# Sliding attention and soft MoE on one core: w1 of experts 0 to 2 loaded as 112 rows and small parts

## The chip, the cores and the metric

The kernel runs on one core of one Trainium2 chip. The metric is the device time of the whole program in microseconds (us), median of several runs, smaller is better. The core's engines go by the profile's names: PE (matmul), PEld (weight load of PE), DVE (vector), ACT (scalar), POOL (GpSimd) and SP (sync). Its transfers are carried by 16 DMA engines.

## The reference

Attention over 8 batches, 8 heads, 576 positions and 64 columns for each head, with two kinds of mask, and behind it a soft mixture of 8 experts with 4 slots each:

```python
def _attn_ref(q, k, v):                       # (8, 8, 576, 64)
    scores = scale * np.matmul(q, k.transpose(0, 1, 3, 2))
    rel = pos[:, None] - pos[None, :]
    mask_plain = (rel >= 0) & (rel < 32)
    mask_dil = (rel >= 0) & (rel < 128) & (rel % 4 == 0)
    ...                                       # heads 0-3 plain, 4-7 dilated
    attn = softmax(where(masks, scores, -1e9))
    return np.matmul(attn, v)

def _moe_ref(x, phi, w1, w2):                 # x (4608, 512), phi (512, 32)
    logits = x @ phi
    d = softmax over rows (axis 0);  slot_input = d.T @ x      # (8, 4, 512)
    for e in range(8):                        # w1 (8, 512, 1024), w2 (8, 1024, 512)
        h = np.maximum(slot_input[e] @ w1[e], 0.0)
        slot_out[e] = h @ w2[e]
    c = softmax over slots (axis 1)
    return c @ slot_out                       # (4608, 512), float32
```

All inputs are float32 in HBM.

## The kernel before, in words

Every large transfer is issued from POOL and turns float32 into float16 on its way in (or float16 into float32 on its way out). One transfer of queries, keys or values is one batch of one of them: 128 partitions of 4608 bytes in float16 (`load_raw`, L197). It lands in a `raw` tile, DVE turns it in blocks of 32 x 32 (L231), and from there on the batch goes through a software pipeline of four stages.

The order of the instructions is written out by hand: `ORDER` (L48) is a list of steps, each with the stage that it belongs to, and the main loop (L540) runs over 11 rounds and in each over the steps. A step such as `S0.0` computes a group of scores, `E0.0` its exponentials on ACT, `MK0.1` the masks on DVE, `AP4.2` the product with the values, `LG.2` and later the logits and the sums of the mixture. Nothing reorders them later; each engine runs its part of this list in order, and waits on semaphores where it needs another's result.

Loads follow the same list. When the second turning step of Q, K or V of batch b is written, `loads` (L527) issues the transfer of batch b + 2 into the tile that has come free. Behind V of batches 3 to 7 one item of `EARLY` (L149) is issued: w1 of expert 0, 1, 2, 3 and 4, each with one transfer (`load_full`, L205). Behind V of batch 7 w1 of experts 5 to 7 and w2 of experts 0 to 2 follow at once. When the last scores are done, w2 of experts 3 to 5 and four pairs of halves of w2 of experts 6 and 7 (`load_half`, L216) are issued into memory that has come free.

A tile of w1 for an expert has 128 partitions. Partition p holds two pieces of 2048 values (u = 0 and u = 1), each of two rows of w1 one behind the other:

```python
in_=moe_w1[e0:e1].rearrange("e (u p c) f -> p (e u) (c f)", u=2, p=128)
```

So a "row" of such a transfer, here and below, is one partition: two runs of 8 KB of float32 in HBM, 4 KB of float16 in the tile.

After the last batch, PE multiplies the slots with w1 (L608), then with w2 (L641). The output is made in halves of columns: `emit_batch` (L681) multiplies with the combine weights (L664), scales on ACT (L673) and DVE (L677), and stores 512 KB at a time (L686); the left-over rows are stored at the end (L713). The first output half needs the first column half of w2 of all experts, the second one the rest.

Transfers use eight completion semaphores in turn; each transfer adds 16 to its semaphore, in 16 steps whose times stand in the trace.

Of the kernel before, what the change touches and what calls it, by code (L numbers as in the profile page):

```python
# [10 lines left out]
FP16 = mybir.dt.float16  # L11
# [16 lines left out]
N_SLOTS = 32  # L28
# [68 lines left out]
def kernel(  # L97
# [10 lines left out]
    nc = tc.nc  # L108
# [5 lines left out]
    consts = ctx.enter_context(tc.tile_pool(name="consts", bufs=1))  # L114
# [3 lines left out]
    ident = cst[:, o : o + 128]  # L118
    spread = cst[:, o + 128 : o + 256]
    quad = cst[:, o + 256 : o + 260]  # L120
    masks = consts.tile([128, NMASK], FP16, name="masks")
    phi_raw = consts.tile([128, 4, N_SLOTS], FP16, name="phi_raw")
    phi4 = consts.tile([128, 4, 4, N_SLOTS], FP16, name="phi4")
# [14 lines left out]
    def weights_tile(pool, which, e0, e1):  # L138
        n = (4 * FDIM, 8 * DMODEL)[which - 1]
        t = pool.tile([128, e1 - e0, n], FP16, name=f"w{which}_{e0}", tag=f"w{which}_{e0}")  # L140
        for e in range(e0, e1):
            of = t[:, e - e0]
            if which == 1:
                w1t[e] = of.rearrange("p (c f) -> p c f", c=4)
            else:
                w2t[e] = of.rearrange("p (c n) -> p c n", c=8)
        return t

    EARLY = [(1, e, e + 1) for e in range(5)] + [(1, 5, 8), (2, 0, 3)]  # L149
    early_tiles = {x: weights_tile((w1_pool, w2a_pool)[x[0] - 1], *x) for x in EARLY}  # L150
# [46 lines left out]
    def load_raw(which, b):  # L197
        t = raw_pool.tile([128, PJ * D], FP16, name=f"raw{which}_{b}", tag=f"raw{which}")
        raw[(which, b)] = t
        src = {"Q": q, "K": k, "V": v}[which][b]  # L200
        nc.gpsimd.dma_start(  # L201
            out=t, in_=src.rearrange("(g h) (p j) d -> (h p) g (j d)", g=2, j=PJ)
        )

    def load_full(t, which, e0, e1):  # L205
        if which == 1:
            nc.gpsimd.dma_start(
                out=t.rearrange("p e (u x) -> p (e u) x", u=2),
                in_=moe_w1[e0:e1].rearrange("e (u p c) f -> p (e u) (c f)", u=2, p=128),
            )  # L210
        else:
            nc.gpsimd.dma_start(
                out=t, in_=moe_w2[e0:e1].rearrange("e (p c) n -> p e (c n)", p=128)
            )

    def load_half(e, s, n):  # L216
# [253 lines left out]
    for which in "QK":  # L470
        load_raw(which, 1)
    nc.gpsimd.dma_start(
        out=phi_raw.rearrange("p (u c) s -> p u (c s)", u=2),
        in_=moe_phi.rearrange("(u p c) s -> p u (c s)", u=2, c=2),
# [8 lines left out]
    def load_weights(n):  # L483
        for _ in range(n):
            x = weights.pop(0)
            load_full(early_tiles[x], *x)

    tmp = {}

# [36 lines left out]

    def loads(which, b):  # L527
        load_raw(which, b)
        if which == "V":
            if b > 2:  # L530
                load_weights(1)
            if b == B - 1:
                load_weights(len(weights))

    frees = {}
# [4 lines left out]
    for it in range(B + max(s for _, s in STEPS)):  # L540
        for op, stage in STEPS:
            b = it - stage
            if not 0 <= b < B:
                continue
            step(op, b)
            if op in frees and b + 2 < B:
                loads(frees[op], b + 2)
            left.discard((op, b))
            if w2b_pool is None and not left:
                raw_pool.release()  # L550
                w2b_pool = tc.alloc_tile_pool(name="w2b", bufs=1, side="right")
                late = weights_tile(w2b_pool, 2, 3, 6)
                slab_weights(6, "qk0", QK_SLAB)
                slab_weights(7, "qk1", QK_SLAB)
                load_full(late, 2, 3, 6)
                for s in range(2):
                    for e in (6, 7):
                        load_half(e, s, 8 if e == 6 else 4)
        if it == 0:
            nc.vector.tensor_copy(  # L560
                out=phi4, in_=phi_raw[:, :, None, :].broadcast_to([128, 4, 4, N_SLOTS])
            )
# [40 lines left out]
    for fc in range(2):  # L603
        for g in range(2):
            for dc in range(4):
                for j in range(4):
                    e = 4 * g + j
# [9 lines left out]
    for c in range(8):  # L617
# [3 lines left out]
        out=hTm[:, 0].rearrange("p c (j s) -> p c j s", j=4)[:, :, :, 0:16], in_=hT4[:, :, :, 0:16]  # L621
    )
    nc.scalar.copy(
        out=hTm[:, 1].rearrange("p c (j s) -> p c j s", j=4)[:, :, :, 16:32], in_=hT4[:, :, :, 16:32]
# [87 lines left out]
    for e in range(2):  # L712
        nc.gpsimd.dma_start(  # L713
            out=rest[:, e, 512:576, :].rearrange("n i d -> i n d"), in_=om_l[64 * e : 64 * e + 64]
# [37 lines left out]
```

## Time and profile before

| | |
|---|---|
| time, median of 3 runs | 178.32 us (178.19 to 178.39) |
| time of the profiled execution | 178.29 us |
| its span | 176.5 us |
| busy: PE, PEld, DVE, ACT, POOL | 123.5, 80.9, 126.0, 123.5, 38.4 us |
| DMA packets | 18981, 40.83 MB as they land, mean 231 GB/s |
| HBM read, written | 62.07 MB, 9.44 MB |
| one transfer of Q, K or V | 576 KB landed, 11.4 to 12.7 us from issue to landing (medians) |
| one transfer of w1 of one expert | 1024 KB landed, 15.9 us from issue to landing |
| outputs in half columns | 512 KB each, 4.6 us from issue to landing |

The span is the time from the first to the last instruction in the profiled execution; the run's time has 1.8 us more around it. The time from issue to landing holds the time in the queue. Bytes are counted as they land, so a weight of float32 counts half of what is read for it. Engines are counted busy only while they compute, or, on POOL, while it writes the descriptors of a transfer.

### The profile page before, as it was taken

To read this page: it belongs to the slowest core of one execution; us is meant where nothing else is said; L and a number is where in the kernel's file an instruction comes from. 1 tells how busy PE (TensorE), PEld (TensorE's weight loads), DVE (VectorE), ACT (ScalarE), POOL (GpSimd) and SP (SyncE) were. 2 spreads that over 40 slices of the span, in tenths; PEclk is the share of its full clock that TensorE was granted. 3 is DMA by queue.
4 is the path that set the end of the run, shared out by engine and by line. 5 is a ranking of instruction groups with operands and counts; after the bars stand their busy time and mean duration, and the time that the engine had idled before them with its cause. 6 is when DMAs were issued, how large, how long until landed. Compare 5 with 4: busy or idle time off the path is not lost.

```text
span 176.5 us, 4724 instructions
## 1 busy us (share of the span) xinstructions
PE 123.5 (70%) x2004; PEld 80.9 (46%) x2004; DVE 126.0 (71%) x275; ACT 123.5 (70%) x266; POOL 38.4 (22%) x60
## 2 busy tenths in 40 slices
PE   0026928998888888988989888978677295778300
PEld 0015616676566566656766557656332142221000
DVE  6473899999999999999999998465130104878500
ACT  6007758999999999999999999995501104888300
POOL 7321022112112112116000002710000001856600
PEclk9999999969999999999789999996858969655555
DMA  5999999999999999999999999999999999999997
GB/s 83 215 214 210 214 212 215 215 213 214 216 212 217 211 218 215 208 215 220 213 211 217 213 218 216 222 210 225 213 213 221 192 198 175 340 398 397 401 415 209
DMA packets 18981, 40.83 MB, mean 231 GB/s; under 512 B 1169, under 2 KB 11537, under 8 KB 18193
## 3 DMA queue, kind: packets, MB, share of 16 engines
q0 software_dynamic: 18816, 40.41, 113.8%
q8 instruction: 15, 0.25, 0.5%
q1 hardware_dynamic: 144, 0.14, 0.3%
q14 instruction: 6, 0.04, 0.1%
HBM read 62.07 MB, written 9.44 MB: 405 GB/s over the span
## 4 chain that ended last, share of the span: by engine, by line
ACT 38%; DMA 27%; DVE 14%; PE 10%; issue 2%; POOL 2%; POOLq 0%; ACTq 0%
DMA w<-in_moe_w_dram 19%; ACT p L282 10%; DMA phi_raw<-in_moe_phi_dram 8%; ACT vX L253 7%; ACT xp L337 7%; DVE qk L231 5%; PE f L664 5%; ACT om L673 3%; ACT xT L376 3%; ACT xT L378 3%; DVE p L293 3%; DVE vT L231 3%; ACT xd L337 2%; PE s L273 2%; PE rp L357 2%
## 5 line engine op out<-in xcount | busy, mean ns | idle before, releaser
L282 ACT ACTIVATE p<-s 128x1920 f16<-128x1920 f32 (+1 forms) x24 | 44.6, 1857 | 10.2 <-PE s L273 10.1
L273 PE MATMUL s<-qk 32*128 32x128 f16 (+2 forms) x704 | 26.7, 295 | 18.4 <-DVE qk L231 12.0
L253 ACT COPY vX<-rv 128x768 f16<-128x768 f16 (+1 forms) x32 | 27.8, 943 | 1.8 <-PE rv L247 1.8
L316 PEld LDWEIGHTS <-p 128*128 128x128 f16 (+1 forms) x480 | 22.4, 103 | 13.3 <-DVE xp L341 4.0
L337 ACT ACTIVATE xp<-o_P,rc_P 128x64 f16<-128x64 f32 x96 | 26.5, 497 | 2.2 <-DVE rc_P L328 2.2
L273 PEld LDWEIGHTS <-qk 32*128 32x128 f16 x704 | 17.3, 117 | 21.6 <-DVE qk L231 12.0
L293 DVE TENSOR_TENSOR p<-p,masks 128x1920 f16<-128x1920 f16 (+1 forms) x24 | 25.7, 1084 | 0.2
L231 DVE STREAM_TRANSPOSE qk<-rawQ 128x576 uint32<-128x576 uint32 x16 | 18.8, 1243 | 2.7 <-DMA rawQ<-in_q_dram 2.7
L316 PE MATMUL o_P<-vX,p 128*128 128x65 f16 (+1 forms) x288 | 20.0, 205 | 0.8 <-ACT xp L337 0.2
L231 DVE STREAM_TRANSPOSE qk<-rawK 128x576 uint32<-128x576 uint32 x16 | 19.5, 1231 | 0.4 <-DMA rawK<-in_k_dram 0.4
L247 PE MATMUL rv<-cst,vT 128*128 128x128 f16 x176 | 17.5, 242 | 3.2 <-DVE vT L231 1.8
L231 DVE STREAM_TRANSPOSE vT<-rawV 128x576 uint32<-128x576 uint32 x16 | 19.4, 1223 | 0.5 <-DMA rawV<-in_v_dram 0.5
L686 POOL DMA_DIRECT2D out_dram<-om x15 | 11.1, 744 | 39.2 <-DVE om L677 34.8
L247 PEld LDWEIGHTS <-vT 128*128 128x128 f16 x176 | 13.2, 124 | 7.5 <-issue 3.7
L677 DVE TENSOR_SCALAR om<-f,rrow 128x256 f16<-128x256 f32 (+1 forms) x28 | 13.5, 519 | 3.5 <-PE f L664 2.9
L664 PE MATMUL f<-so_sb,ET 32*128 32x256 f16 (+1 forms) x60 | 12.5, 392 | 3.9 <-ACT om L673 2.7
L673 ACT ACTIVATE om<-f,rrow 128x256 f16<-128x256 f32 (+1 forms) x28 | 12.8, 503 | 2.6 <-PE f L664 2.0
L376 ACT COPY xT<-rp 128x576 f16<-128x576 f16 x16 | 11.5, 909 | 1.3 <-PE rp L357 1.3
L316 PE MATMUL o_D<-vX,p 128*128 128x65 f16 x128 | 9.9, 202 | 2.5 <-DVE xp L341 2.0
L201 POOL DMA_DIRECT2D rawQ<-in_q_dram x8 | 5.1, 633 | 29.4 <-DVE rc_P L328 18.4
L378 ACT COPY xT<-rd 128x576 f16<-128x576 f16 x16 | 10.6, 795 | 0.0
L341 DVE TENSOR_TENSOR xd<-o_D,rc_D 128x256 f16<-128x256 f32 x24 | 9.9, 412 | 0.2
(81 smaller groups left out, 176.7 us busy)
## 6 DMA issues: line engine op xcount, KB each, us to landing
w<-in_moe_w_dram POOLq DMA_DIRECT2D x3, 3072.0 KB, 35.5
out_dram<-om POOLq DMA_DIRECT2D x11, 512.0 KB, 4.6
w<-in_moe_w_dram POOLq DMA_DIRECT2D x5, 1024.0 KB, 15.9
rawQ<-in_q_dram POOLq DMA_DIRECT2D x8, 576.0 KB, 12.7
rawK<-in_k_dram POOLq DMA_DIRECT2D x8, 576.0 KB, 11.4
rawV<-in_v_dram POOLq DMA_DIRECT2D x8, 576.0 KB, 11.6
out_dram<-om POOLq DMA_DIRECT2D x2, 1024.0 KB, 7.3
w<-in_moe_w_dram POOLq DMA_DIRECT2D x2, 512.0 KB, 36.7
```

The source lines that it names most:

```text
L231: nc.vector.transpose(out=out_, in_=in_)
L247: nc.tensor.transpose(rg[:, n_t, :, c, :], rows, ident)
L253: copy(out=vX[b % 2][:, t0 : t0 + n, :, 0:D], in_=rg.rearrange("p n h c d -> p n h (c d)"))
L273: nc.tensor.matmul(sps[:, h, c0 : c0 + w], kk, qq, start=(tt == 0), stop=(tt == 1))
L282: return nc.scalar.activation(out=pt, in_=sps[:, :, 0:n], func=AF.Exp, scale=SCALE)
L293: return nc.vector.tensor_tensor(out=pt, in0=pt, in1=m, op=ALU.mult)
L316: nc.tensor.matmul(o[rows, h, :], lhs, rhs, start=(n == 0), stop=(n == len(jobs) - 1), skip_group_check=True,)
L337: nc.scalar.activation(out=dst[:, h], in_=src[:, h], func=AF.Copy, scale=rc[:, h : h + 1])
L376: copy(out=xT_t[b][:, c, :], in_=rg[:, 0:S])
L378: copy(out=xT_t[b][:, 2 + c, :].rearrange("p (i r) -> p i r", r=DIL), in_=rg[:, :, 0:SUB].rearrange("p r i -> p i r"),)
L664: nc.tensor.matmul(fp[:, 0 : c1 - c0], ET[32 * j : 32 * j + 32, m : m + 128], so_sb[32 * j : 32 * j + 32, c0:c1], start=True, stop=True,)
L673: nc.scalar.activation(out=dst, in_=fp[:, 0 : c1 - c0], func=AF.Copy, scale=rrow[:, blk : blk + 1])
```

## The change

w1 of experts 0, 1 and 2 is no longer one transfer each. `load_pieces` issues the first 112 partitions as one transfer, and for expert 0 also the half u = 1 of the other 16. What remains is put on a list, `pieces`, from which `loads` takes one each time that it has issued a transfer of Q, K or V:

- expert 0: the halves u = 0 of partitions 112 to 127, in four transfers of 8, 4, 2 and 2 partitions, behind Q, K and V of batch 4 and Q of batch 5
- expert 1: partitions 112 to 119 and 120 to 127, behind K and V of batch 5
- expert 2: partitions 112 to 119 behind Q of batch 6 and 120 to 127 behind V of batch 6, and a `step_cursor` after each of them, behind K of batch 6 and Q of batch 7

`step_cursor` loads from eight rows of phi two runs of 32 values each into a new small tile, `aside`, which nothing reads. Every byte of w1 is still loaded once, to the same place.

```diff
+    aside = consts.tile([16, 3, 2, N_SLOTS + 16], FP16, name="aside")
...
+    def step_cursor(i, n):
+        nc.gpsimd.dma_start(
+            out=aside[0:n, i, :, 0:N_SLOTS],
+            in_=moe_phi[0 : 5 * n].rearrange("(p u) s -> p u s", u=5)[:, 0:4:2, :],
+        )
+
+    pieces = []
+
+    def load_pieces(t, e):
+        src = moe_w1[e].rearrange("(u p c) f -> p u (c f)", u=2, p=128)
+        dst = t[:, 0].rearrange("p (u x) -> p u x", u=2)
+        nc.gpsimd.dma_start(out=dst[0:112], in_=src[0:112])
+
+        def piece(p, n, u=None):
+            if u is None:
+                return lambda: nc.gpsimd.dma_start(out=dst[p : p + n], in_=src[p : p + n])
+            return lambda: nc.gpsimd.dma_start(out=dst[p : p + n, u], in_=src[p : p + n, u])
+
+        if e == 0:
+            nc.gpsimd.dma_start(out=dst[112:128, 1], in_=src[112:128, 1])
+            p = 112
+            for n in (8, 4, 2, 2):
+                pieces.append(piece(p, n, 0))
+                p += n
+        elif e == 1:
+            pieces.extend((piece(112, 8), piece(120, 8)))
+        else:
+            pieces.extend(
+                (piece(112, 8), lambda: step_cursor(0, 8), piece(120, 8), lambda: step_cursor(1, 8))
+            )
...
             x = weights.pop(0)
-            load_full(early_tiles[x], *x)
+            if x[0] == 1 and x[1] < 3:
+                load_pieces(early_tiles[x], x[1])
+            else:
+                load_full(early_tiles[x], *x)
...
         load_raw(which, b)
+        if pieces:
+            pieces.pop(0)()
         if which == "V":
             if b > 2:
                 load_weights(1)
             if b == B - 1:
+                while pieces:
+                    pieces.pop(0)()
                 load_weights(len(weights))
```

## The prediction

> **What bounds the kernel now.** I read the sliced page first, to see which resource is busy throughout, then the chain of waits, then the DMA queues, and last the single packets and completions that the trace keeps for each transfer.
>
> ```profile
> DVE  6473899999999999999999998465130104878500
> ACT  6007758999999999999999999995501104888300
> ...
> DMA  5999999999999999999999999999999999999997
> ```
>
> Each digit is a slice of 4.4 us. The DMA engines are at 90% or more in 38 of 40 slices, also where ACT falls off (from slice 27, 119 us).
>
> ```profile
> 109.68 1.62 PE s L273 x24
> 111.30 0.28 issue
> 111.58 0.74 POOL w L220
> 112.33 34.05 DMA w<-in_moe_w_dram
> 146.37 0.04 issue
> 146.41 0.32 PE so L641 x4
> ...
> 165.69 0.65 issue
> 166.34 0.63 POOL out_dram L713
> ```
>
> The chain (start, length, what) spends 34.05 us in one small transfer of w2. It isn't a long transfer: it stands behind the backlog of weights. So from 4 us to 151.7 us the kernel is one stream of loads, and what ends it is the last of 16 DMA engines.
>
> ```profile
> PE so L641 <- DMA w<-in_moe_w_dram: 3.0, 2, 2.3
> ...
> DVE qk L231 <- DMA rawQ<-in_q_dram: 2.7, 1, 2.7
> ```
>
> In the table of waits (total us, times, longest) the compute engines wait for loads only at the very start and for the last weights. V of batch 7 lands at 92.0 us and is first read at 102.7; V of batch 3 lands at 38.3, and its first transpose is at 50.5. Queries, keys and values have over 10 us to spare.
>
> ```profile
> q0 software_dynamic: 18816, 40.41, 113.8%
> q8 instruction: 15, 0.25, 0.5%
> ...
> q14 instruction: 6, 0.04, 0.1%
> ```
>
> The instruction fetches on q8 look like nothing (0.5%), but each is one packet of 16 KB on one engine. Their starts are 22.3, 33.4, 42.7, 48.9, 57.0, 65.0, 72.1, 80.2, 86.1 ... 144.8 us, and they take 0.89 to 1.07 us. The 16 completion times that every transfer leaves show what they do. K of batch 1 (landed 17.9) completes on its 16 engines within 0.41 us. After the first fetch, one engine is 0.7 us behind the rest (26.4 to 27.1); after the eighth, eight are about 1 us behind (82.6 to 83.0 against 81.4 to 82.1). The ninth and later ones hit the same eight again. The last weight transfer completes at 149.0 to 150.2 us on nine engines and at 151.3 to 151.7 on seven. So eight engines carry all the fetches, seven twice, and are up to 2.66 us late; the others are free, and idle until the first output packet at 150.68.
>
> What follows is DMA-bound too: 9.4 MB of output in 512 KB transfers that land every 1.32 us, 4 to 5 us after their issue. The late engines run without a pause from 151.70 to the last landing at 175.23. The span (176.5) ends 1.3 us behind it, and the run's own time is 178.29, 0.03 below the median of three (178.32).
>
> **The change, part by part.**
>
> *Bytes and rows.* Each expert's w1 is 128 rows of two packets (2048 packets of 4096 B for eight experts: 16 on each engine for each expert, eight rows). 112 rows are seven for each engine. What matters is where the other 16 go. For expert 0 the 16 half rows, then 8, 4, 2 and 2 half rows are 16 twice over. If a transfer of n rows takes n engines, and the next one goes on where it stopped, every engine gets its eighth row. Expert 1 with 8 and 8 is the same. Expert 2 differs: 8 rows, then eight rows of phi into a tile that nothing reads, then 8 rows, then phi again. By the same assumption both 8-row parts fall on the same eight engines, which get two rows, and the other eight none. No transfer before shows under 16 engines, so this placement is the unknown; its cases are priced below.
>
> By the Trainium skill ("DMA: Bandwidth & Descriptors", "Why a DMA increments its semaphore by 16 and not by 1"), a GpSimd transfer whose slowest dimension is 8 takes eight consecutive engines from a round-robin cursor, and one with 16 takes all. No run so far shows this.
>
> *Is it the late eight that are spared?* If the first part starts at the first engine, the first eight get more. Which are late isn't named, but the packet list gives a hint. Around 151 us the early engines write 1024-byte output packets while the late ones still load 512-byte ones. Of 23 neighbouring pairs of these two kinds with the same start in ns, the early engine's stands first in 20. A list kept by engine number would give that if the late ones are the upper eight (the one engine of them with a single fetch being nearly on time). So I take it that the upper eight are relieved.
>
> *Price.* In steady state 4096-byte packets start 0.305 us apart on an engine (they take 0.324 and overlap by 0.019). One row less is 2 x 0.305 = -0.61 us on each late engine, +0.61 on the early ones. Reading a row's price from 0.65 (two whole packets) gives -0.65 at most.
>
> *Added transfers.* Expert 0 goes from one to six, expert 1 to three, expert 2 to five: 11 more. Each ends in a completion packet on every engine, 22 ns: eight packets of a Q load at 0.342 and this 22 make 2.758, and loads land 2.76 apart. 11 x 0.022 = +0.24 us. If engines outside a part had no completion it would be five on a late engine, 0.11; with the longest completion packets among loads (42 ns) 0.46. I take 0.24, as all transfers of the trace complete 16 times. The phi steps are two packets each, of the kind that in the phi load start 13 ns apart: 4 x 13 = +0.05 on the engines that are stepped over, the late ones. The phi load itself, 32 KB in small packets, moved the stream by 0.26 us (17.89 to 18.15), so a small transfer in a full queue has no large fixed cost.
>
> Against the change stands a rule of the Trainium skill (same page, "Anatomy of one DMA"): a fixed cost of about 2.0 us for each GpSimd transfer. In series that would be an estimated 22 us more, some 200 us; the phi row speaks against it, since the queue is never empty here.
>
> *POOL.* A load of Q, K or V keeps POOL 0.59 us, one of w1 0.79. Eleven more issues are 6.5 to 8.7 us on an engine that is 22% busy and idle 2.0 to 4.7 us before each load. Each part follows a load; behind it wait the next load, 2 to 5 us away, and on V the weights, 0.6 us later into a backlog of over 8 us. Eight completion semaphores are used in turn, so w1 of expert 1 may have to wait some 1.6 us for expert 0's 112 rows (landing near 43.2); next behind it is Q of batch 5, at 46.5. All of it costs nothing; were that cover gone, it would be 0.6 us for each part. The delayed rows are first used at 130 us.
>
> *Sum.* -0.61 + 0.24 + 0.05 = -0.32 us on the late engines. Next in line are the early ones: the latest of them ends its weights at 150.2, and 0.61 + 0.24 more is 151.07, still before the late ones' 151.38. The last half of w2 for the first output columns lands on late engines (146.37) and comes 0.32 earlier, so the first output issue (149.40) does too, and the whole output stage moves. 178.29 - 0.32 = 177.97; on the median, 178.0. With the bounds, 177.8 to 178.2.
>
> **Rivals.**
>
> *The wrong eight (slower).* If the first 8-row part of expert 2 falls on the late eight, because the upper eight aren't the late ones or the counting doesn't start at the first engine, each late engine gains a row: +0.61 + 0.24 = +0.85, 179.15. It decides at that one transfer. For it: the trace names no engine, and nothing shows where the count stands. Against: the order of the pairs above.
>
> *No shift.* Parts are spread over all engines, or the steps don't step. Then only the added packets are left, +0.24 to +0.29: 178.6. For it: every transfer shown uses all 16 engines.
>
> *Always from the first engine.* If n rows go to engines 0 to n-1 each time, the upper eight lose 0.5 + 1 + 1 = 2.5 rows (-1.52 us), and the first two gain 1.5 + 1 + 1 = 3.5 (+2.13). With completions these two end at 149.0 to 150.2 + 2.37 = 151.4 to 152.6 instead of the late ones' 151.7: 178.0 to 179.2, middle 178.5. The Trainium skill has, in the section named above, an exception of this kind: some direct copies go over all 16 engines with the rounded-up sixteenth of the partitions on each, so that the last ones stay empty.
>
> *Small transfers in series:* far slower; the phi row leaves little for it.
>
> **How the numbers follow.** Forecast case 0.58, wrong eight 0.21, no shift 0.10, from the first engine 0.08, other slower 0.03. 0.2%, about what a measurement of this kernel can tell from no change, is 0.36 us, and the forecast of -0.32 lies just inside. Its two added terms could be smaller, so I give 0.31 of its 0.58 to faster and 0.27 to same. No shift: 0.06 same, 0.04 slower. First engine: 0.02, 0.03, 0.03. Together faster 0.33, same 0.36, slower 0.31. The likeliest case has 177.8 to 178.2 for itself; with no shift and the first engine that is under 8 in 10, so the range reaches into the wrong eight: 177.8 to 179.2.
>
> **What would show it.** Right: the last weight transfer's 16 completions span about 1.5 us instead of 2.66, their last is near 151.4, V of batch 7 lands within 0.4 us of before, the q0 packets grow by 11 x 16 completions (and 32 of phi), and POOL's waits change nothing. Wrong: a span of nearly 4 us (wrong eight), one unchanged at 2.7 with all of it 0.25 later (no shift), two engines alone at the end (first engine), or idle slices in the DMA row.

## The result, and the profile after

The change is slower: 178.82 us (median of 11 runs, 178.67 to 179.76) against 178.36 us for the kernel before (11 runs, 177.99 to 178.45), ratio 1.0034, 95% interval 1.0021 to 1.0047. The forecast was 178.0, a gain of 0.32; it came out as a loss of 0.46. The profiled execution after took 178.94 us (before 178.29) at a span of 177.2 us (before 176.5).

The sliced part of the page and the DMA queues of the changed kernel:

```profile
DMA  5999999999999999999999999999999999999997
```

```profile
q0 software_dynamic: 19168, 40.41, 113.6%
q8 instruction: 15, 0.25, 0.5%
...
q14 instruction: 5, 0.04, 0.1%
```

The load stream is as full as before, with the same 15 instruction fetches on q8. Queue q0 has 352 packets more. 32 are the steps' packets of phi; 176 are the completions of eleven more transfers, 16 each, as forecast. The other 144 were not foreseen: completion packets that short transfers leave beyond sixteen (see the last section).

The chain of work that ended last (start, length, what) and a row of the table of waits (total, times, longest):

```profile
111.20 0.74 POOL w L252
111.95 35.19 DMA w<-in_moe_w_dram
147.13 0.04 issue
147.18 0.32 PE so L680 x4
...
167.06 0.64 POOL out_dram L752
```

```profile
PE so L680 <- DMA w<-in_moe_w_dram: 4.3, 2, 2.9
```

The same transfer of w2 carries the chain. It was issued 0.38 us earlier than before (111.95 against 112.33) and landed 0.76 later (147.13 against 146.37), and PE's longest wait for it grew from 2.3 to 2.9 us. The first output is issued at 150.18 instead of 149.40, and the last landing moves from 175.23 to 175.82, by 0.59. So the loss is there before the output begins; what comes behind only follows.

Where in the stream it is shows in the 16 completions of the last weight transfer, from the trace's completion times (us, sorted):

```
before  149.04 .24 .25 .31 .33 .59 .81 150.18 .22 | 151.27 .29 .38 .42 .43 .50 .70           mean 150.37
after   148.33 .41 149.36 .85 150.00 .45 .51 .52 .66 .72 .78 .96 151.22 .53 | 152.11 .13     mean 150.47
```

The span grew from 2.66 to 3.80 us, instead of shrinking to 1.5. The late group of seven is gone: most engines now end between 149.4 and 151.5. But two stand alone at 152.11 and 152.13, and two are far too early. The mean is only 0.10 later. To that comes a shift that the change didn't make: the twelve transfers of Q, K and V of batches 0 to 3, all landed before any row is moved, complete 0.10 us earlier here than in the trace of before. Counted from its own start of the stream, the mean is 0.20 later, and that is the whole price of eleven more transfers. The work was hardly made longer, it was put on some wrong engines.

POOL around the first parts and expert 1's 112 rows (start, length; in brackets the idle time before and what ended it):

```profile
37.66 0.59 POOL L202 DMA_DIRECT2D rawK<-in_k_dram  x1 [3.03 <-DVE rc_P L360]
38.20 0.56 POOL L233 DMA_DIRECT2D w<-in_moe_w_dram  x1
...
43.16 0.71 POOL L228 DMA_DIRECT2D w<-in_moe_w_dram  x1 [1.82 <-DMA w<-in_moe_w_dram]
46.19 0.59 POOL L202 DMA_DIRECT2D rawQ<-in_q_dram  x1 [2.32 <-DVE rc_P L360]
```

A part costs POOL 0.56 us here, and the new wait for a completion semaphore is there: 1.82 us, ahead of expert 1's 112 rows. Q of batch 5 is issued 3.03 us after it and has to wait for DVE anyway. V of batch 7 lands at 91.9 us (before 92.0). So POOL is not the cause.

### The profile page after: what moved, and what is told of

Read it like the earlier page. It is cut to its first block, busy times and chain, and to the rows that moved or that the text cites. A ratio compares the mean times of both kernels' runs of the same rounds, so it can differ in the third digit from the quotient of the medians.

```text
span 177.2 us, 4744 instructions
## 1 busy us (share of the span) xinstructions
PE 122.4 (69%) x2004; PEld 82.4 (47%) x2004; DVE 125.9 (71%) x275; ACT 123.3 (70%) x266; POOL 44.4 (25%) x71
## 4 chain that ended last, share of the span: by engine, by line
ACT 38%; DMA 28%; DVE 14%; PE 10%; issue 3%; POOL 2%; POOLq 0%; ACTq 0%
DMA w<-in_moe_w_dram 20%; ACT p L314 10%; DMA phi_raw<-in_moe_phi_dram 8%; ACT vX L285 7%; ACT xp L369 7%; DVE qk L263 5%; PE f L703 5%; ACT om L712 3%; ACT xT L408 3%; ACT xT L410 3%; DVE p L325 3%; DVE vT L263 3%; ACT xd L369 2%; PE s L305 2%; PE rp L389 2%
```

## The experiments

The question was which engines get the parts of 2 to 16 rows, and which engines are the late ones. Each ratio is against the kernel before, timed with it on the same chip. "Late engine" means one of the seven that end the last weight transfer at 151.27 to 151.70 before the change. The parts' names (`load_pieces`, `step_cursor`, `piece`) are those of the change; kernels that split one expert leave the others as one transfer. The trace names no engine: the numbers 0 to 15 count from where the first part of whole rows, or the first step, of a kernel falls, and that place is taken to be engine 0.

One thing has to be taken off before completions of two traces are compared. The stream of loads doesn't start at the same time in each execution. "Start" below is the mean completion of the twelve transfers of batches 0 to 3, as a difference to the trace of before; it lies between -0.10 and +0.32 us, and no kernel has moved a row by then. Already the first load of Q completes at 6.60 us (mean of 16) before, at 6.50 with the change and at 6.87 in the kernel with parts on 6 to 13. Completions are given as the traces have them.

**One part of the change at a time, and two checks of placement.** Expert 1 alone:

```diff
-            if x[0] == 1 and x[1] < 3:
+            if x[0] == 1 and x[1] == 1:
```

> Expert 1 alone is split, into 112 rows and two parts of 8 rows; experts 0 and 2 are loaded whole. Theory F (every small part starts at the first engine, so that 8 rows always go to the same lower eight engines): the upper eight lose one row (0.61 us), the lower eight gain one; the last weight transfer's latest completion goes from 151.70 to about 151.1, the early engines end at 150.9 at the latest, and the time is 177.8 (0.6 below before). Theory C (the parts go round the engines, as the forecast had it): balanced, only two more completions, 178.4. Theory N (parts are spread evenly, added transfers cost time): 178.4 as well.

Measured: 178.31 us against 178.33, ratio 1.0001 (0.9992 to 1.0010). The last completions are those of before: nine to 150.36, then seven at 151.27 to 151.64. If both 8-row parts had fallen on the same eight engines, these would have gained a row and the others lost one. So theory F is out: the second part went on where the first had stopped (C), or both were spread over all engines (N), which expert 2 alone rules out below.

Expert 0 alone:

```diff
-            if x[0] == 1 and x[1] < 3:
+            if x[0] == 1 and x[1] == 0:
```

> Expert 0 alone is split, into 112 rows, 16 half rows, and 8, 4, 2 and 2 half rows; experts 1 and 2 are loaded whole. Theory F: the first two engines gain 1.5 rows (0.92 us) and end at 151.3 at the latest, the upper eight lose half a row (0.31): latest completion about 151.5, time 178.15, 0.2 below before. Theory C: all balanced, five more completions, 178.45. Theory N: the same 178.45.

Measured: 178.20 us against 178.33, ratio 0.9991 (0.9982 to 0.9999). The completions are 148.82 to 150.71 on nine engines and 151.05 to 151.30 on seven: the late group came 0.3 earlier, some of the others up to 0.5 later. So expert 0 is not balanced. Its parts are half rows; 0.305 us is just the one packet that a late engine has less if the 8, 4, 2 and 2 half rows all start at the first engine each time, so that they stay on the first eight. That start is inferred; no run shows it engine by engine.

Expert 1 as 112 rows and eight parts of 2 rows:

```diff
-            pieces.extend((piece(112, 8), piece(120, 8)))
+            pieces.extend(piece(p, 2) for p in range(112, 128, 2))
```

> Expert 1 alone is split, into 112 rows and eight parts of two rows, one behind each of the next eight transfers of queries, keys and values. Theory F: the first two engines carry all 16 rows, seven more than their own (+4.3 us), and stand alone at the end of the weights, at 153.5 to 154.7 with all others at 151.1 or before; time 180.2 to 181.4. Theory C: the eight parts go once round the 16 engines, balanced, 178.5. Theory N: 178.5.

Measured: 178.51 us in one run. Completions 149.08 to 150.35 and 151.34 to 151.73: balanced again. This fits eight parts of two whole rows that go once around the sixteen engines. The Trainium skill ("DMA: Bandwidth & Descriptors", "Why a DMA increments its semaphore by 16 and not by 1") has this rule for GpSimd transfers: k consecutive engines from a round-robin cursor. These completions agree with it. Its exception fits the half rows of expert 0 (late group 0.3 us earlier): some direct copies are dealt out over all sixteen engines with the rounded-up sixteenth of their partitions for each. With fewer than 16 partitions that would leave the last engines without any.

Only more transfers, no shift: w1 of experts 0 to 4 as 112 rows and two transfers of 16 half rows, ten transfers more.

```diff
+        pieces.extend((piece(112, 16, 0), piece(112, 16, 1)))
...
-            if x[0] == 1 and x[1] < 3:
+            if x[0] == 1 and x[1] < 5:
```

> Experts 0 to 4 are each split into 112 rows and two parts of 16 half rows that follow the transfers of queries, keys and values: ten more transfers, one short of the change, and each of them on all 16 engines. No theory sees a shift of rows here. What is left is the price of the transfers: 10 x 22 ns on each engine, 178.6, if the prediction's row holds; 178.45 if the 0.10 us by which the mean completion of the last weights moved with the change is all that eleven transfers cost. Above 178.9, the added transfers and not the rows would explain the change's loss.

Measured: 178.61 us (178.26 to 179.33), ratio 1.0019 (1.0008 to 1.0029). The mean completion is 150.48, 0.11 later than before; the start is 0.07 earlier, so ten transfers cost 0.18 us in the stream. The last completion is 151.64, and the late and the early group stand as before. The time is 0.28 longer; ten completion packets of 22 ns are 0.22. The Trainium skill (same page, "Anatomy of one DMA") gives each such transfer a fixed cost of about 2.0 us. As a delay of the stream it isn't there: 0.18 us for ten.

**Expert 2, and the count moved.** Expert 2 alone (`x[1] == 2`):

> Expert 2 alone is split, as in the change: 8 rows, a step of eight, 8 rows, a step of eight; experts 0 and 1 are loaded whole. Parts of whole rows go round the engines from the first (expert 1 alone was balanced), so engines 0 to 7 get one row more and 8 to 15 one less. Theory U (the late eight are 8 to 15, as the prediction had it): -0.61 + 0.1 on all late engines, 177.85. Theory S (the late eight are 6 to 13, so that two of them lie among the first eight): engines 6 and 7 go from 151.4 to about 152.1 and stand alone at the end of the weights, engines 14 and 15 end near 148.5; time 178.7 to 178.9, about the change's own.

Measured: 178.76 us against 178.54, ratio 1.0016 (1.0006 to 1.0026). Completions 148.76 and 148.81, then thirteen from 149.88 to 151.42, then 152.01. So the parts are not spread evenly. This one split already has the look of the change: two engines too early and one too late. The chain:

```profile
112.62 34.20 DMA w<-in_moe_w_dram
146.86 0.32 PE so L680 x4
```

PE starts at 146.86 instead of 146.41, 0.45 later; the change's 147.18 is 0.77 later.

The next three move the count with steps of phi, so that expert 2's two 8-row parts fall on another eight engines. The time before on their chip is 178.54 us. The first set of eight is 14, 15 and 0 to 5:

```diff
-                (piece(112, 8), lambda: step_cursor(0, 8), piece(120, 8), lambda: step_cursor(1, 8))
+                (lambda: step_cursor(0, 14), piece(112, 8), lambda: step_cursor(1, 8), piece(120, 8), lambda: step_cursor(2, 10))
```

> Expert 2 alone is split; a step of 14 rows comes before the first part of 8, a step of eight between the parts, a step of ten behind them. Both parts then fall on engines 14, 15 and 0 to 5. Theory S: these are just the eight without instruction fetches; all late engines lose a row, the latest completion is near 151.2 and the early ones end at 150.9 at the latest; time 177.8 to 177.95, faster than before by some 0.45. Theory U: engines 14 and 15 are late ones and gain a row: latest completion 152.2, time 178.8.

Measured: 178.82 us, ratio 1.0023 (1.0013 to 1.0033). The gain of theory S did not come; two engines stand alone, at 152.20 and 152.42, as theory U had it. A gain needed all the late ones to be among engines 6 to 13.

The mirror image, steps of 6, 8 and 2, with the parts on engines 6 to 13:

> Expert 2 alone is split; steps of six, eight and two rows. Both parts fall on engines 6 to 13. Theory S: all eight late engines gain a row: latest completion 152.3 to 152.4, and seven engines stand together at the end instead of two; time 179.0. Theory U: six of the eight are late ones (8 to 13): six engines at the end, and two at about 150.8 that were late before; time 179.0 too. What differs is the number of engines in the late group.

Measured: 179.21 us, ratio 1.0039 (1.0024 to 1.0054). Six engines end together at 152.29 to 152.82, all others by 151.34. The chain:

```profile
112.47 35.08 DMA w<-in_moe_w_dram
147.59 0.32 PE so L680 x4
```

Six engines ended with a row more. PE starts 1.18 us later than before, where a row (0.61) and five added transfers (0.10) make 0.71. Of the rest, 0.32 is this execution's own later start: the mean of the last completions is 0.42 later, which is 0.10 without it. Some 0.15 stays unexplained.

Steps of 12, 8 and 12, the parts on engines 12 to 15 and 0 to 3:

> Expert 2 alone is split; steps of twelve, eight and twelve rows. Both parts fall on engines 12 to 15 and 0 to 3. Theory S: of these only 12 and 13 are late ones, so two engines end alone at about 152.2: 178.8. Theory U: 12 to 15 are late ones, four engines (or three) end at about 152.2: 178.8. The time is the same, the number of engines in the latest group tells them apart.

Measured: 179.21 us, ratio 1.0045 (1.0028 to 1.0061), with three engines alone at 152.16 to 152.38. The completions are where theory U had them. The time is 0.67 longer than before on this chip, where both theories had some 0.5 (178.8 against 178.32). No set of eight that was tried holds all the late ones. How many of them a set holds is counted by how many stand at the end: one on 0 to 7 (expert 2 alone), six on 6 to 13, three on 12 to 3, two on 14 to 5.

**A map by fours.** Expert 1 as 112 rows and four parts of 4 rows, all on the same four engines: between them lie steps of 12 rows of phi. These four engines get three rows more, the other twelve one less.

```diff
+        pieces.extend(
+            (piece(112, 4), lambda: step_cursor(0, 12), piece(116, 4), lambda: step_cursor(1, 12), piece(120, 4), lambda: step_cursor(2, 12), piece(124, 4), lambda: step_cursor(3, 12))
+        )
```

> Of expert 1 alone, 112 rows are loaded at once; the other 16 follow as four parts of 4 rows, and behind each part 12 rows of phi (read by nobody) that move the count on, so that all four parts fall on engines 0 to 3. These get three rows more (3 x 0.61 = +1.83 us), the other twelve one less (-0.61). Theory M (the engines that carry the instruction fetches are none of 0 to 3, two of 4 to 7, three of 8 to 11, three of 12 to 15): the late ones all lose 0.61, and the last weight transfer's 16 completions end four engines near 151.0 to 152.1 and all others before 151.3; output end -0.5 to 0 us, time 177.9 to 178.5. Theory U (the late ones are the upper eight, as in the prediction): the same here, since the upper eight are relieved too. If the count doesn't stand at the first engine: some late engine near 153.3, time near 180.

> The same with one step of 4 rows of phi ahead of the first part, so that the four parts fall on engines 4 to 7. Theory M: exactly two engines end alone near 151.4 + 1.83 = 153.2 to 153.5 in the last weight transfer, two more near 151 to 152, the other twelve 0.61 earlier than before; time +1.3 to +1.9 us, 179.7 to 180.2. Theory U: no engine beyond 152.1, time 177.9 to 178.5 as with engines 0 to 3.

> The same with a step of 8, so that the parts fall on engines 8 to 11. Theory M: three engines end alone near 153.2 to 153.5 and one near 151 to 152; time 179.7 to 180.2. Theory U: four engines near 153.3, time 179.7 to 180.2.

> The same with a step of 12, so that the parts fall on engines 12 to 15. Theory M: three engines end alone near 153.2 to 153.5 and one near 151 to 152; time 179.7 to 180.2. Theory U: four engines near 153.3, time 179.7 to 180.2.

Measured, against 178.41 us before: engines 0 to 3 178.88 (ratio 1.0028, 1.0017 to 1.0039), 4 to 7 179.97 (1.0085, 1.0071 to 1.0099), 8 to 11 180.00 (1.0089, 1.0075 to 1.0103), 12 to 15 180.25 (1.0104, 1.0088 to 1.0119). The last completions:

```
0-3    148.69 ... 149.84 | 150.91 .93 .99 151.01 .06 .09 .10 .20 .45 .74 152.17
4-7    148.71 ... 149.84 | 150.91 .96 .98 .99 151.08 .11 .26 .38 | 152.13 | 153.51
8-11   148.67 ... 149.91 | 150.91 .96 151.03 .04 .07 | 153.34 .35 .41
12-15  148.85 ... 149.94 | 150.98 151.12 .15 .40 .42 | 153.63 .76 154.02
```

The seven late engines of before have a mean of 151.43. Three rows more are 1.83, the eight added transfers some 0.2: about 153.4. So many engines end at 153.34 or later: none for 0 to 3, one for 4 to 7 (theory M had two), three for 8 to 11, three for 12 to 15. That is all seven. A second engine among 4 to 7 ends at 152.13. By this count the order of the packet list, on which the forecast rested, was right for six of the late engines and wrong for the seventh, and one engine is enough. The same by the chain of waits, for the parts on engines 4 to 7 and on 12 to 15:

```profile
112.16 35.89 DMA w<-in_moe_w_dram
148.05 0.04 issue
148.09 0.32 PE so L671 x4
```

```profile
113.42 35.25 DMA w<-in_moe_w_dram
148.67 0.04 issue
148.71 0.32 PE so L671 x4
```

The transfer that carries the chain lands at 148.05 and 148.67 instead of 146.37: one overloaded engine costs nearly what three do. For engines 0 to 3 the placement came as expected and the time did not: an engine that isn't late itself ends at 152.17 with three rows more. The expectation had 151.0 to 152.1 for it and still forecast no loss, although the latest before is 151.70; the range of the time should have gone to +0.5.

**A smaller dose, and the change without expert 0.** Expert 0 as 112 rows, 16 half rows, and four parts of 4 half rows, which need no step:

```diff
-            for n in (8, 4, 2, 2):
+            for n in (4, 4, 4, 4):
```

> Expert 0 alone: 112 rows, 16 half rows, and then the other 16 half rows as four parts of 4, which need no step if each starts at the first engine. Engines 0 to 3 then carry three packets of 4096 bytes more (3 x 0.305 = +0.92 us), the other twelve one less (-0.31). Theory M (no late engine among 0 to 3): the late ones end their weights at 151.70 - 0.31 + 0.07 = 151.45, engines 0 to 3 at 149.3 to 150.2 + 0.99 = at most 151.2, so nobody comes after the late ones; time 0.1 to 0.3 us less than before. If half-row parts follow the count instead of starting at the first engine, the load is even and the time is that of before plus 0.1 to 0.2. If engines 0 to 3 hold a late one: an engine alone near 152.6, time +0.5 to +0.9.

Measured: 178.16 us against 178.27, ratio 0.9995 (0.9986 to 1.0004): no difference that this measurement can tell. The load is uneven, eight engines at 148.79 to 150.58 and eight at 150.88 to 151.67, so these parts don't follow the count. But the last completion is 151.67, not 151.45, and the chain starts where it did before:

```profile
113.51 32.83 DMA w<-in_moe_w_dram
146.38 0.32 PE so L680 x4
```

The forecast gain isn't shown. Which engines end at 151.63 and 151.67 can't be read from the completions.

The change with expert 0 left as one transfer (`x[1] in (1, 2)`):

> The change without expert 0's part: experts 1 and 2 as in the change. Theory M (the end of the change is set by the late engine among 4 to 7 that expert 2's parts load with one row more; expert 0 relieves only engines that aren't last): the last weight completion at 152.0 to 152.2 as in the change, one engine alone instead of two, the time within 0.2 us of the change's, 178.6 to 178.9. Rival (expert 0's parts are the ones that cost): the time of before, 178.3 to 178.5.

Measured: 178.72 us, ratio 1.0034 (1.0021 to 1.0047), the same ratio as the whole change. Two engines stand alone, at 152.01 and 152.05. So expert 0's parts have no share in the loss that this measurement can tell; its interval is 0.23 us to either side. The second of the two late ones isn't expert 0's doing either: the expectation had one engine alone and was wrong there.

**The kernels in one table.** The start of the stream (as defined above), the landing of the last half of w2 for the first output columns (w2), the last weight completion, and the end of the output, from one trace each; the change in time is of the median, against the median of before on the same chip (parts of two rows: one run):

```
                start   w2       last weight   end of output   end - last   time
before           0      146.37   151.70        175.23          23.5          0
expert 0        -0.04   146.44   151.30        175.13          23.8         -0.13
half0           +0.02   146.34   151.67        175.20          23.5         -0.11
expert 1         0.00   146.32   151.64        175.18          23.5         -0.02
two rows        -0.09   146.72   151.73        175.39          23.7         +0.18
sixteens        -0.07   146.72   151.64        175.41          23.8         +0.28
expert 2        +0.06   146.82   152.01        175.56          23.6         +0.22
1 and 2         +0.03   146.70   152.05        175.60          23.6         +0.45
the change      -0.10   147.13   152.13        175.82          23.7         +0.46
fours on 0-3    +0.01   146.87   152.17        175.69          23.5         +0.47
parts on 12-3   +0.11   147.10   152.38        175.91          23.5         +0.67
parts on 14-5   +0.13   147.15   152.42        175.96          23.5         +0.28
parts on 6-13   +0.32   147.55   152.82        176.36          23.5         +0.67
fours on 4-7    -0.04   148.05   153.51        176.87          23.4         +1.56
fours on 8-11   -0.03   148.05   153.41        176.88          23.5         +1.59
fours on 12-15  +0.15   148.67   154.02        177.49          23.5         +1.84
```

The output ends 23.4 to 23.8 us after the last weight completion in every one of them. Within one execution the end is that of the latest DMA engine; the medians of the time follow it less closely, to within some 0.5 us, since a trace is a single execution with a start of its own.

## Why the prediction was wrong

*What failed: "is it the late eight that are spared?"* The prediction took the upper eight as the late ones, from 20 of 23 neighbouring packets. By the fours, six of the seven late engines are in 8 to 15 and one in 4 to 7. Expert 2's 8-row parts fell on engines 0 to 7, as its part by part working said (expert 2 alone: one engine late, two too early), so six late engines were relieved and one was loaded. With the mean of the late engines, the price of a row and the 0.20 of the added transfers, that one ends at 151.43 + 0.61 + 0.20 = 152.24. The change's last completion is 152.13, which is 152.23 by the start of before. That it fits to 0.01 is luck: a late engine may be 0.2 from the mean. This accounts for one of the two engines that stand at the end. The closest rival was the wrong eight, whose mechanism acted on one or two engines, where it had all the late ones: since the latest engine alone decides, that was enough for most of its loss. It forecast +0.85; the trace's end moved by 0.59, the time by 0.46. By the list of completions the gain would have been small even without these two: the next engine of the change ends at 151.53, where the prediction had 151.38 for the last.

*Expert 0 "the same, balanced": wrong, without consequence.* Its half-row parts don't go on where the last one stopped. Alone that gives 0.13 us to the good; inside the change no effect of it can be told.

*A row's price, 0.61: right.* Three rows more on 8 to 11 moved three engines by 1.94, against 1.83 and some 0.2 for the added transfers. With the parts on 6 to 13 the last completion moved by 1.12, of which 0.32 is that execution's later start; 0.80 stays against 0.71.

*Added transfers, +0.24: right, slightly high.* The mean completion rose by 0.10 for eleven (the change) and by 0.11 for ten. With the earlier start of both executions taken off, that is 0.20 and 0.18, or 18 ns each; the time of the ten rose by 0.28. The packets behind it were not all foreseen: 144 on top of the 176.

*POOL, its semaphore, Q, K and V: right.* A part costs 0.56 us, close to the forecast, and V of batch 7 lands no later (91.9 us).

*Late engines, then output: right, and the most useful step.* The output ends 23.4 to 23.8 us behind the last engine in every trace.

Still open: which engine the second late one of the change is, and why it is late. Among 4 to 7 one engine carries a late engine's full lateness and a second, at 152.13 in the fours, does not; yet with experts 1 and 2 split two engines stand within 0.04 us of each other, and with expert 2 alone one. Parts on 14 to 5 had two late engines where the counts of the other sets leave one. All traces have the same 15 fetches on q8, so their number doesn't explain it.

## What to carry to other kernels

When one stream of transfers fills all DMA engines, the end is that of the latest engine, and a rebalancing pays only if no late engine is among those that get more: here one or two mistaken engines of sixteen cost the whole gain. Before rows are moved by hand, map the late engines with short transfers on four engines at a time, and read the spread of a late transfer's completions, not the mean load. Take off first what the traces differ by before the change acts: here that was up to 0.32 us, as much as the gain that was forecast. Check also where parts of each shape go, since two ways of cutting the same rows were placed by different rules.

## What the runs showed of the hardware

- The instruction fetches, 0.5% of the DMA time on the page, go with seven of sixteen engines being up to 2.66 us late. That rests on the trace of before, where one more engine falls behind after each of the first eight fetches; no run changed the fetches. The late engines don't form a block: none of engines 0 to 3, one of 4 to 7, three each of 8 to 11 and 12 to 15, counted as above.
- Whole-row parts of 2, 4 and 8 rows behave as if they went to as many consecutive engines and carried a count onward across transfers: eight parts of 2 rows leave the late group at 151.34 to 151.73, and the four sets of fours load none, one, three and three late engines. Parts of 8, 4, 2 and 2 half rows don't (late group 0.3 us earlier), though they move rows of the same tile.
- Short transfers leave more than sixteen completion packets of 4 bytes. Expert 1 alone has 64 packets more on q0 than before: two more transfers make 32, and each of its 8-row parts 16 beyond that, two for each engine that it doesn't use. Eight parts of 2 rows leave 224 beyond their sixteens, which is 28 each, again two for each of 14 idle engines. Expert 0's half-row parts leave 48 beyond their sixteens, one for each engine that 8, 4, 2 and 2 leave idle.

```profile
q0 software_dynamic: 18880, 40.41, 113.9%
```

(expert 1 alone; before 18816.)
